# Issuing the loads of V from ScalarE's DMA queue instead of SyncE's, two of a period side by side

## The chip, the cores and the metric

One core of one Trainium2 chip runs the whole kernel. The metric is the device time of one execution in microseconds (us), so less is better. Engines are named as in the profile: PE is TensorE (PEld its weight loads), DVE is VectorE, ACT is ScalarE, POOL is GpSimd and SP is SyncE. A q behind an engine's name (SPq, ACTq) means its instruction queue, the sequencer that issues DMAs and waits for semaphores. The profile numbers the DMA queues: q1 holds what SP issues, q10 what ACT issues, and q8 is a queue of instruction fetches.

## What is computed

Two independent blocks A and B with the same shapes, whose results stand side by side in the output. In each, a projected query attends to a given K and V cache, and the heads are projected back:

```python
B, Sq, D = 16, 64, 640
H, Sk, Dh = 32, 512, 128
q = (x @ wq).reshape(B, Sq, H, Dh).transpose(0, 2, 1, 3)
scores = jnp.einsum("bhqd,bhkd->bhqk", q, k_cache) * (Dh ** -0.5)
p = softmax(scores, axis=-1)
o = jnp.einsum("bhqk,bhkd->bhqd", p, v_cache)
out = o.transpose(0, 2, 1, 3).reshape(B, Sq, H * Dh) @ wo
```

Everything is bf16. K and V of both blocks together take 256 loads of K and 256 loads of V, 512 KiB each, which is nearly all of the 292 MB that the kernel reads.

## The kernel before

The work is cut into 256 steps of two heads and two batches (an index m from 0 to 255); two steps make a *period*, of which there are 128. A period needs two loads of K (`kn_ring`, 9 slots) and two loads of V (`v_ring`, 5 slots of two halves: a period's two loads are the two batches of four heads). On top of that come the loads of the weights (`wq_sb`, `wo_sb`, 16 each, 640 KiB) and of x.

The order of every engine's instructions is written out by hand in `Cfg.PHASES`: for each engine a list of operations with an offset in steps and a time within the period. `build_plan` turns each into an `Op` with a time `ts`, in units of steps, and sorts each engine's list by it. An engine executes its list in that order. The operations that this document speaks of are

- on PE: `KX` transposes K (line 586), `QN` projects the queries of later steps (L603), `SM` computes the scores (L632), `TR2` transposes the probabilities (L670), `PV2` multiplies them with V (L694), `OP2` and `OX` project the output (L709, L719), `XT` transposes x (L804);
- on ACT: `EX` is the exponential with its row sum (L647, an ACTIVATE and a READ_ACCUMULATOR), `QEN` and `TA2` copy PSUM to SBUF (L619, L684), `OE4` copies the result of four PV products (L701), `OVP`, `OXP` and `XTE` are small copies (L727, L732, L833), and `ST` issues the DMA that stores a block of the output (L748), 16 times in all;
- on DVE: `MX` takes the row maximum (L641), `KE` and `TE2` copy (L593, L680); on POOL: `NM` normalizes the probabilities (L661).

A period of ACT runs OE4, EX, EX, EX, QEN, TA2, EX, and then the OE4 of the next one. OE4 waits for the second PV2 of the period, which is the last thing on PE in it; the first EX after it waits for DVE's MX.

Loads are ordered by the planner at the end of `build_plan` (lines 332 to 385). Each load gets a key, the time at which it may start: `LEAD` (5.37 steps) or `WLEAD` ahead of its first reader, and not before the slot is free. Sorted by that key, all loads go to SP's list (L384), K, V, x and weights mixed. The planner also computes, from estimated DMA costs, when the queue would come to each load, and takes the PE operation that runs at that time, but at the latest the one that runs `BEFORE` (3.88 steps) ahead of the load's first reader:

```python
i = bisect.bisect_right(pe_us, min(t_now, us(first - cfg.BEFORE))) - 1
if i > 0:
    paced.append((op, progs["pe"][i]))
```

`paced` makes the load wait for that PE operation: SP doesn't issue it until PE has come so far. So PE's progress paces the whole DMA queue. `em_LDKV` (L782) emits a load of K (L792) or V (L789). `prune_waits` leaves out each wait that another one implies. Each slot of a ring has a DMA semaphore of its own, on which PE waits before it reads the slot.

Of the kernel before, what the change touches and what calls it, by code (L numbers as in the profile page):

```python
# [15 lines left out]
class Cfg:  # L16
# [97 lines left out]
    OXH = False  # L114
    KTB = (6, 6)
    NWU = 32


class Op:
# [20 lines left out]
def build_plan(dims, cfg):  # L140
# [23 lines left out]
    progs = {e: [] for e in ENGINES}  # L164

    def mk(eng, kind, idx, reads, writes, ts, aux=None, dur=0.0):
        return Op(eng, kind, idx, reads, writes, dur=dur, aux=aux, ts=ts)
# [18 lines left out]
    for k in range(NPER - PPQ):  # L186
        u, i, hc = k // PPQ, k % PPQ // HG, k % HG
# [127 lines left out]
    for n, (k_lo, *templates) in enumerate(cfg.PHASES):  # L315
        k_hi = cfg.PHASES[n + 1][0] if n + 1 < len(cfg.PHASES) else 0
        for eng, template in zip(("pe", "act", "dve", "pool"), templates):
            for kind, off, sub, t in template:
                for m in range(2 * (k_lo % NPER) + off % 2, 2 * (k_hi % NPER or NPER), 2):
                    op = make_op(kind, m, sub, m - off + 2 * t / cfg.PERIOD)  # L320
# [8 lines left out]

    progs["pe"] = [mk("pe", "WU", -1, [("ident",)], [], -99, aux=cfg.NWU)] + progs["pe"]  # L330

# [6 lines left out]
    for ps_ in range(NPASS):  # L338
        for j in range(HG):
            ready = []  # L340
            if ps_:
                first = ("QN", (2 * ps_ - 1) * MPQ + j * MPG, 0)
                ready = [("QN", (2 * ps_ - 2) * MPQ + j * MPG + MPG - 2, 0)]
            else:
                first = ("QZ", 2 * j - 2, 0 if j > 1 else G) if j else ("QJ", 0, 0)
            add(ready, first, cfg.WLEAD, 0, "LDWQ", (ps_, j), [("wq", qslot(j))], (ps_, j))
            i = ps_ * HG + j
# [21 lines left out]
    def us(t):  # L369
        us_, a = min(t, 0) * cfg.STEP_US[0][1], 0  # L370
        for b, step in cfg.STEP_US:
            us_ += step * max(0, min(t, b) - a)
            a = b
        return us_

    pe_us = [us(op.ts) for op in progs["pe"]]
    paced = []
    t_now = cfg.START_US
    for key, first, _, op in sorted(loads, key=lambda e: e[:3]):
        t_now = max(t_now, us(key))  # L380
        i = bisect.bisect_right(pe_us, min(t_now, us(first - cfg.BEFORE))) - 1
        if i > 0:
            paced.append((op, progs["pe"][i]))
        progs["sp"].append(op)  # L384
        t_now += cfg.DMA_US[op.kind] * (op.aux[2] - op.aux[1] if op.kind == "LDX" else 1)

    counts = {}

    def sem_key(op):
# [113 lines left out]
def mha_kernel(nc, blocks, out, cfg=None):  # L503
# [12 lines left out]
    N1 = DN - N0  # L516

    progs, info = build_plan(dict(NBLK=NBLK, B=B, H=H, KT=KT), cfg)
    prune_waits(progs)
    NBP, SPB, NHALF = info["NBP"], info["SPB"], info["NHALF"]  # L520
# [413 lines left out]
```

## Time and profile before

| | |
|---|---|
| Median of 3 runs | 853.83 us (850.14 to 856.91) |
| The profiled execution's own time | 852.97 us |
| Its span (first to last instruction) | 851.0 us |
| Mean granted TensorE clock | 0.998 |
| DVE, ACT and POOL busy | 727.9, 644.7 and 417.1 us |
| Read from HBM | 292.03 MB, of which V is 134.2 MB |

The span is what the profiler sees; the 2 us beside it lie around it. The page's slices are 40 equal parts of the span, about 21 us each. "Released by" or "<-" behind an idle time names what ended the wait. "issue" is idle time in which the engine waited for nothing that the profile shows.

### The profile page before, as it was taken

How to read it: one execution, taken by the hardware profiler on the slowest of the kernel's cores; microseconds unless marked ns; L12 is line 12 of the kernel's file. 1: busy time of each engine (PE TensorE's matmuls, PEld its weight loads, DVE VectorE, ACT ScalarE, POOL GpSimd, SP SyncE). 2: the span in 40 equal slices, each digit the busy share in tenths (PEclk: the TensorE clock that was granted, in tenths of full speed). 3: DMA queues.
4: the chain of work that ended last, by engine and by line, in shares of the span. 5: the costliest groups of instructions: out<-in, count | busy, mean ns of one | idle time of the engine just before them, and what ended most of it. 6: DMA issues, size and time to landing. Idle time of an engine off the chain costs nothing.

```text
span 851.0 us, 38366 instructions
## 1 busy us (share of the span) xinstructions
PE 811.3 (95%) x17025; PEld 566.4 (67%) x17156; DVE 727.9 (86%) x1192; ACT 644.7 (76%) x1466; POOL 417.1 (49%) x518
## 2 busy tenths in 40 slices
PE   8999999999999999999999998999999999999996
PEld 5566676666666666666666666666666666666664
DVE  4688888888888898888899887988888989989994
ACT  2678877777777787777877877787887877778886
POOL 0355455454544554454554545455455455455553
PEclk9999999999999999999999999999999999999999
DMA  9999999999999999999999999999999999999992
GB/s 306 360 354 349 369 354 352 348 338 362 354 352 353 369 369 363 359 360 367 364 362 367 364 360 349 321 362 362 360 360 363 366 369 365 366 339 352 370 321 89
DMA packets 228438, 297.14 MB, mean 349 GB/s; under 512 B 9136, under 2 KB 162736, under 8 KB 228272
## 3 DMA queue, kind: packets, MB, share of 16 engines
q1 hardware_dynamic: 225968, 292.06, 100.3%
q8 instruction: 134, 2.20, 1.1%
q10 hardware_dynamic: 2304, 2.62, 0.9%
q14 instruction: 32, 0.26, 0.1%
HBM read 292.03 MB, written 2.62 MB: 346 GB/s over the span
## 4 chain that ended last, share of the span: by engine, by line
PE 89%; issue 3%; ACT 3%; DMA 2%; DVE 2%; SPq 0%; ACTq 0%
PE ps L586 17%; PE ps L694 15%; PE ps L603 15%; PE ps L632 14%; PE ps L670 13%; PE ps L709 12%; PE ps L719 3%; ACT p_ring L647 2%; DMA v_ring<-in_A_v_cache_dram 1%; DVE negmax L641 1%; ACT pT_ring L684 1%; DMA wq_sb<-in_A_wq_dram 1%; DVE ktp_ring L593 1%; PE ps L804 0%; PE ps L813 0%
## 5 line engine op out<-in xcount | busy, mean ns | idle before, releaser
L661 POOL TENSOR_SCALAR pn_ring<-p_ring,recip 128x512 bf16<-128x512 bf16 x512 | 416.4, 843 | 425.1 <-DVE recip L653 379.0
L647 ACT ACTIVATE p_ring<-ps,negmax 128x512 bf16<-128x512 f32 x512 | 349.0, 688 | 74.0 <-DVE negmax L641 68.5
L593 DVE COPY ktp_ring<-ps 128x2048 bf16<-128x2048 bf16 x256 | 312.1, 1219 | 56.3 <-PE ps L586 56.2
L641 DVE TENSOR_REDUCE negmax<-ps 128x1 f32<-128x512 f32 x512 | 328.3, 683 | 16.2 <-PE ps L632 8.5
L586 PEld LDWEIGHTS ps<-ident,kn_ring 64*128 64x128 bf16 x8192 | 136.8, 95 | 107.9 <-issue 96.4
L586 PE MATMUL ps<-ident,kn_ring 64*128 64x64 bf16 x8192 | 169.2, 191 | 3.3 <-issue 1.4
L603 PE MATMUL ps<-xT_sb,wq_sb 128*128 128x512 bf16 (+2 forms) x543 | 133.4, 372 | 19.0 <-issue 18.1
L670 PEld LDWEIGHTS ps<-ident,pn_ring 128*128 128x128 bf16 x2048 | 125.4, 98 | 38.8 <-ACT p_ring L647 7.2
L694 PE MATMUL ps<-pT_ring,v_ring 128*128 128x64 bf16 x4096 | 143.5, 194 | 2.8 <-issue 1.9
L701 ACT ACTIVATE oT_ring<-ps 128x512 bf16<-128x512 f32 x128 | 76.4, 597 | 91.7 <-PE ps L694 91.7
L684 ACT ACTIVATE pT_ring<-ps 128x1024 bf16<-128x1024 bf16 (+1 forms) x144 | 140.9, 987 | 3.0 <-DVE pT_ring L680 2.2
L670 PE MATMUL ps<-ident,pn_ring 128*128 128x128 bf16 x2048 | 138.9, 219 | 3.4 <-issue 1.6
L709 PE MATMUL ps<-wo_sb,oT_ring 128*128 128x512 bf16 x498 | 135.3, 379 | 4.0 <-issue 1.9
L632 PE MATMUL ps<-ktp_ring,qc_ring 128*64 128x512 bf16 x1024 | 135.5, 385 | 0.7 <-issue 0.7
L694 PEld LDWEIGHTS ps<-pT_ring,v_ring 128*128 128x128 bf16 x4096 | 128.2, 98 | 9.6 <-issue 2.4
L647 ACT ACTIVATION_READ_ACCUMULATOR p_ring<-ps,negmax 128x1 f32 x512 | 104.8, 205 | 0.0
L680 DVE COPY pT_ring<-ps 128x1024 bf16<-128x1024 bf16 (+1 forms) x128 | 82.5, 644 | 14.6 <-PE ps L670 14.1
L619 ACT ACTIVATE qc_ring<-ps 128x512 bf16<-128x512 f32 (+1 forms) x129 | 76.8, 596 | 21.5 <-PE ps L603 21.4
L603 PEld LDWEIGHTS ps<-xT_sb,wq_sb 128*128 128x128 bf16 x660 | 53.8, 98 | 54.0 <-issue 1.1
L632 PEld LDWEIGHTS ps<-ktp_ring,qc_ring 128*64 128x64 bf16 x1024 | 47.2, 109 | 34.1 <-issue 1.3
L709 PEld LDWEIGHTS ps<-wo_sb,oT_ring 128*128 128x128 bf16 x512 | 42.7, 98 | 25.0 <-ACT pT_ring L684 2.1
L653 DVE RECIPROCAL recip<-rowsum 128x2 f32<-128x2 f32 x256 | 39.8, 155 | 4.4 <-ACT p_ring L647 4.4
(21 smaller groups left out, 127.2 us busy)
## 6 DMA issues: line engine op xcount, KB each, us to landing
kn_ring<-in_A_k_cache_dram SPq DMA_DIRECT2D x128, 512.0 KB, 6.5
v_ring<-in_A_v_cache_dram SPq DMA_DIRECT2D x128, 512.0 KB, 6.8
kn_ring<-in_B_k_cache_dram SPq DMA_DIRECT2D x128, 512.0 KB, 6.3
v_ring<-in_B_v_cache_dram SPq DMA_DIRECT2D x128, 512.0 KB, 6.5
wq_sb<-in_A_wq_dram SPq DMA_DIRECT2D x8, 640.0 KB, 7.1
wo_sb<-in_A_wo_dram SPq DMA_DIRECT2D x8, 640.0 KB, 7.2
wq_sb<-in_B_wq_dram SPq DMA_DIRECT2D x8, 640.0 KB, 6.8
wo_sb<-in_B_wo_dram SPq DMA_DIRECT2D x8, 640.0 KB, 6.6
```

The source lines that it names most:

```text
L586: last = e.transpose(kt_ps[hs][:, 64 * t:64 * t + 64], kn_ring[r, m % NKB, t // 8, t % 8 * DH:(t % 8 + 1) * DH], ident[r, r])
L593: ins = e.tensor_copy(ktp_ring[:, ktslot(op.idx)], ps[:, b:b + 2, :].rearrange("p b s -> p (b s)").bitcast(BF16))
L603: last = e.matmul(dst[:, col:col + n], wq_sb[:, qslot(hh // G), kt, (hh % G) * DH:(hh % G + 1) * DH], xT_sb[:, kt, lo * 128:hi * 128], sta ...
L632: ins = e.matmul(s_bank(g)[64 * j:64 * j + 64, :], q[:, 64 * j:64 * j + 64], kt[:, sub, j], start=True, stop=True, tile_position=(0, 64 * j))
L641: ins = e.reduce_max(negmax[:, r:r + 1], s_bank(g), axis=AX.X, negate=True)
L647: ins = e.activation(p_ring[:, g % NP, :], s_bank(g), ACTF.Exp, bias=negmax[:, r:r + 1], scale=1.0, accum_out=rowsum[:, r:r + 1])
L661: ins = e.tensor_scalar(dst, src, recip[:, r:r + 1], 1.0, ALU.mult, ALU.mult)
L670: ins = e.transpose(pt_flat(m)[:, (4 * sub + t) * 128:(4 * sub + t + 1) * 128], pn_ring[:, g % NPN, t * 128:(t + 1) * 128], ident[:, :])
L680: ins = e.tensor_copy(*pt_copy(op.idx, op.aux))
L684: ins = e.activation(*pt_copy(op.idx, op.aux), ACTF.Copy)
L694: ins = e.matmul(qo_ps[:, col:col + 64], v_ring[:, m // 2 % NVP, j, 2 * (m % 2) + sub, t * DH:(t + 1) * DH], pT_ring[:, m % NT, sub, t, 64 ...
L709: ins = e.matmul(out_ps, oT_ring[:, m // 2 % NO, 2 * (m % 2) + sub, :], wo_sb[:, wslot(ps_, hh // G), hh % G, 0:N0], start=(hh == 0), stop ...
```

## The change

Loads of V (kind `LDV`) are no longer put on SP's list. They become operations of ACT, with a time of their own, and ACT's list is sorted again with them in it. K, x and the weights stay on SP as they are, in the same order and with the same waits.

```diff
+    VFIRST = 12
...
     for key, first, _, op in sorted(loads, key=lambda e: e[:3]):
         t_now = max(t_now, us(key))
         i = bisect.bisect_right(pe_us, min(t_now, us(first - cfg.BEFORE))) - 1
-        if i > 0:
-            paced.append((op, progs["pe"][i]))
-        progs["sp"].append(op)
+        if op.kind == "LDV":
+
+            op.eng = "act"
+            t = progs["pe"][max(i, cfg.VFIRST)].ts
+            op.ts = min(first - 0.01, max(key, t) if t < 4 else 2 * round(t / 2) + 0.02)
+            progs["act"].append(op)
+        else:
+            if i > 0:
+                paced.append((op, progs["pe"][i]))
+            progs["sp"].append(op)
         t_now += cfg.DMA_US[op.kind] * (op.aux[2] - op.aux[1] if op.kind == "LDX" else 1)
+    progs["act"].sort(key=lambda o: o.ts)
```

The time of a load of V is that of the PE operation that would have paced it, rounded to the nearest start of a period (an even number of steps) plus 0.02. Loads of V carry no paced wait; what holds them back is their place in ACT's list. In the built program that place is behind the last EX of a period and ahead of OE4 (or of the ST ahead of it) in 125 of 128 places. The lists of PE, DVE and POOL are unchanged. Counted in the built program, 96 places have two loads, 16 have three and 16 have one, and none of the 256 loads carries a wait for a semaphore: what ACT waited for earlier implies that the slot is free.

## The prediction

> **What bounds the kernel now.** First the page's busy times, slices and queues, then who waited for whom.
>
> ```profile
> span 851.0 us, 38366 instructions
> PE 811.3 (95%) x17025; PEld 566.4 (67%) x17156; DVE 727.9 (86%) x1192; ACT 644.7 (76%) x1466; POOL 417.1 (49%) x518
> ...
> DMA  9999999999999999999999999999999999999992
> GB/s 306 360 354 349 369 354 352 348 338 362 354 352 353 369 369 363 359 360 367 364 362 367 364 360 349 321 362 362 360 360 363 366 369 365 366 339 352 370 321 89
> ...
> q1 hardware_dynamic: 225968, 292.06, 100.3%
> q8 instruction: 134, 2.20, 1.1%
> q10 hardware_dynamic: 2304, 2.62, 0.9%
> ```
>
> Two things are full at once: PE is busy 95% of the span, and SP's queue q1 keeps the 16 DMA engines busy all the time at 350 to 369 GB/s. The waits say which one holds the other up:
>
> ```profile
> ACT oT_ring L701 <- PE ps L694: 91.7, 121, 1.8
> ACT p_ring L647 <- DVE negmax L641: 68.5, 127, 0.8
> ...
> PE ps L586 <- DMA v_ring<-in_A_v_cache_dram: 0.7, 1, 0.7
> ```
>
> PE waits for a load of V once, 0.7 us, just before its first use of V at 33.7 us, and never again. So DMA runs at its limit but PE sets the time. I cut the trace at the end of each second PV2. 74 periods have a QN and neither OX nor XT: the shortest is 6.11 us and so is their median. The 28 with an OX have 7.00 and 7.01. All time above the shortest of its class sums to 13.1 us from 57 us on; that and the first 34 us are all a better DMA could give back.
>
> More than half of the 13.1 us are gaps in the middle of an operation where nothing is waited for. In the chain that ended last, near 530 us:
>
> ```profile
> 529.18 0.69 PE ps L694 x20
> 529.87 1.06 issue
> 530.92 0.51 PE ps L694 x12
> ```
>
> PE stops after 20 of 32 matmuls. There are 12 such gaps between 160 and 835 us, 7.0 us together. They fit instruction fetch: q8 moved 134 packets of 16 KB for the 34181 instructions of PE and PEld, 255 each, the gaps stand at multiples of that, and 11 of the 12 end 1.32 to 1.62 us after a q8 packet ended.
>
> **The change part by part.** The sum is made against the profiled execution's own 852.97 us, 0.86 below the median of 853.83.
>
> *256 issues leave SP.* SP only issues, so its freed time is worth nothing. Loads of K lose no wait of their own.
>
> *256 issues join ACT, behind the last EX of a period.* One costs 0.34 to 0.44 us in the 16 rows of L748. In SP's rows, the second of two issues less than 0.1 us apart has a median of 0.47 and a mean of 0.61 us (71 cases after 40 us, longest 1.52). A pair then takes 0.37 + 0.04 + 0.47 = 0.88 us, a triple about 1.4. Does ACT's engine stand still meanwhile? This row of the ACT timeline decides:
>
> ```profile
> 788.88 0.69 ACT L647 ACTIVATE p_ring<-ps,negmax 128x512 bf16<-128x512 f32 x1
> 788.89 0.34 ACTq L748 DMA_DIRECT2D out_dram<-out_sb  x1
> 789.47 0.19 ACT L647 ACTIVATION_READ_ACCUMULATOR p_ring<-ps,negmax 128x1 f32 x1
> 789.75 0.60 ACT L701 ACTIVATE oT_ring<-ps 128x512 bf16<-128x512 f32 x1
> ```
>
> With nothing to wait for, the queue issues while EX runs; the same is seen at 812.67 and 835.92. Loads of V carry no wait and stand behind the same EX, so the first 0.8 us of a pair lie under it. Then come two idle times in every plain period:
>
> ```profile
> 624.25 0.71 ACT L647 ACTIVATE p_ring<-ps,negmax 128x512 bf16<-128x512 f32 x1
> 624.82 0.23 ACT L647 ACTIVATION_READ_ACCUMULATOR p_ring<-ps,negmax 128x1 f32 x1
> 625.85 0.60 ACT L701 ACTIVATE oT_ring<-ps 128x512 bf16<-128x512 f32 x1 [0.80 <-PE ps L694]
> ```
>
> 0.80 us before OE4, and 0.53 between OE4 and EX (which waits for DVE). Behind these wait QN (it needs OE4's bank; OE4 is done 0.70 us before) and TR2 (it needs EX's bank; behind an ST this EX starts 0.20 to 0.27 us later and the period takes 6.24, so about 0.1 us is to spare). Cover is 0.80 + 0.80 + 0.53 = 2.1 us; after an OX or XT it is about 1.6. Even a triple fits. I take 0. If the cover under EX is gone, the excess of pairs and triples over the two idle times, summed place by place, is 8.8 us with a second issue of 0.47 and 15.6 with 0.60. Bounds: 0 and +15.6.
>
> *The start.* V's first two loads are issued by SP at 15.8 and 21.9 us and land at 27.1 and 33.6; PV2 wants them at 32.7. On ACT they go out near 15.5. The 0.7 us wait goes; next in line are a K and a WQ load that land 3.2 and 3.7 us ahead of their readers, while 1 MB of V, 2 x 1.45 us at the rate at which landings follow each other, cuts in. That fits. I take -0.7; bounds -0.9 (all of that wait) and +1.
>
> *V's loads meet K's in the DMA engines.* In before, a load takes 6.3 to 6.8 us from issue to landing, in order. When an ST runs on q10, the packet records show its 1280-byte packets 94 ns apart beside q1's 1024-byte ones, where the two take 55 and 46: the engines alternate single packets of the two queues and lose nothing. In a pair each engine has 64 packets of V. Beside a period's 40 of K and weights (84 ns for K's 2048 bytes) that is 64 x 0.046 + 40 x 0.084 = 6.3 us, plus about 2.5 us from issue to first packet (2.1 to 3.3 for the STs under load): 8.8 us. By where ACT and PE stand in this trace, two thirds of V's loads will go out 10.8 to 13.3 us before their PV2, a sixth 18 or more, 12 of 256 less than 10.8. For most, 2 us and more are left: I take 0. If every packet of V had one of K beside it, 64 x 0.130 + 2.5 = 10.8 us, and the 34 periods with a lead under 11.6 would be at the edge; 0.35 us in each is +12. Bounds: 0 and +12.
>
> *Instruction fetch.* From the trace, a q8 packet starts on average 2.9 us after PE enters the block ahead of it (0.2 to 5.2), against 0.3 at the first fetch. With the spare time of each of the 126 fetches, extra latency costs: 0.2 us more, 5.6 us in all; 0.3, 9.4; 0.5, 18.7; 1.0, 50. Less latency gives up to 7.0 back. In the fetches during STs the latency is 1.5 to 4.0, as elsewhere, so I take 0; but an ST has 9 packets per engine, a pair of V 64. Bounds: -7.0 and +50. [...]
>
> Sum: 852.97 - 0.7 + 0 + 0 + 0 = 852.3 us.
>
> **The rivals.**
>
> *Instruction fetch falls behind (slower).* If each queue keeps packets of its own in flight inside an engine, a fetch waits behind those of two queues. For: latency is ten times that of the first fetch, and margins are thin. Against: STs don't show it. It decides from +0.3 us of latency on (+9.4 us); my price is +0.5: 852.3 + 18.7 = 871.0, and 902 at +1.0.
> [...]
>
> *ACT's issues aren't covered (slower).* [...] +8.8 to +15.6: 861 to 868. Against: the row at 788.88.
>
> *V comes late (slower).* As above, +12: 864.
>
> *Two queues feed the engines better (faster).* During STs both queues together move 340 to 380 GB/s, mostly over 360, against 350 to 364 in most 100 us windows. Then fetches come sooner, and of the 13.1 us above the shortest periods some goes; all of it would give 852.3 - 13.1 = 839.2. 844.4 needs 60% of it. Against: DVE and ACT waits in there have nothing to do with DMA.
>
> [...]
>
> **How the numbers follow.** My forecast, all four terms small, 0.45 (own range 846 to 860). Fetch 0.20, ACT uncovered 0.10, V late 0.12, faster 0.13. Within 1% is 844.4 to 861.5, about what a measurement of this kernel can tell from no change. Faster by over 1%: 0.13. Within: 0.45 plus 0.02 of the uncovered ACT at its lower price, 0.47. Slower: the rest, 0.40. The range 843 to 875 takes in the forecast, both cheap rivals and fetch to +0.6 us; left out are a dearer fetch (about 0.12) and the deepest gain (0.05).
>
> **What would show it.** After: q10 with about 137 MB; issues of V on ACTq inside EX's time; 0.80 before OE4 still there, or smaller where issues are long. "DMA v_ring" among PE's waits means V comes late. More or longer "issue" gaps inside PE's operations, or periods over 6.11 with no other wait, mean fetch. "ACT oT_ring L701" idle by "issue" means ACT isn't covered. I am wrong if a full second queue does to fetches what an ST's few packets can't.

## The result, and the profile after

| | before | after |
|---|---|---|
| Median | 851.99 us | 877.56 us (873.88 to 882.2, 4 runs) |
| Ratio, with its 95% interval | 1 | 1.0297 (1.0219 to 1.0374) |
| The profiled execution's own time | 852.97 us | 875.14 us |
| Its span | 851.0 us | 873.1 us |

The median of before is that of the runs beside the changed kernel. The change costs 3.0%, against a forecast of no change. The changed kernel's lines stand nine further down: PV2 is L703, KX L595, QN L612, EX L656, OE4 L710, ST L757 and the load of V L798.

The page of the changed kernel, busy times, slices and queues:

```profile
span 873.1 us, 38366 instructions
PE 817.6 (94%) x17025; PEld 568.2 (65%) x17156; DVE 728.8 (83%) x1192; ACT 645.3 (74%) x1466; POOL 418.1 (48%) x518
...
GB/s 271 364 333 352 353 325 342 358 366 354 343 353 352 326 348 369 354 325 365 355 356 362 367 346 361 325 336 334 353 354 350 359 351 330 372 338 340 370 312 89
...
q1 hardware_dynamic: 90800, 157.83, 52.0%
q10 hardware_dynamic: 137472, 136.86, 47.5%
q8 instruction: 134, 2.20, 1.1%
```

The change did what it says: q10 now moves 137 MB. The work of ACT, DVE and POOL is nearly unchanged (ACT 645.3 against 644.7 us). PE is busy 6.3 us longer, about half of it, by the estimate for cut operations below, at the cuts. DMA still moves up to 372 GB/s, but from the second to the 38th slice nine are under 340, where before has three. So most of the time lost isn't work. Where does PE stand still? The waits of the changed kernel (engine, line, releaser: us in total, times, longest):

```profile
ACT oT_ring L710 <- issue: 8.5, 7, 2.0
PE ps L703 <- issue: 6.9, 12, 1.4
PE ps L595 <- issue: 6.8, 19, 1.0
...
PE ps L612 <- ACT oT_ring L710: 2.3, 4, 1.0
PE ps L718 <- ACT oT_ring L710: 2.2, 3, 1.2
...
PE ps L703 <- DMA v_ring<-in_B_v_cache_dram: 0.3, 1, 0.3
```

The same lines of before:

```profile
PE ps L694 <- issue: 1.9, 3, 1.1
...
PE ps L586 <- issue: 1.4, 5, 0.5
...
PE ps L709 <- ACT oT_ring L701: 0.7, 1, 0.7
```

PE's stops for "issue" in PV2 and KX grew from 3.3 to 13.7 us, its waits for OE4 from 0.7 to 4.5 us, and V is late once. The first kind in the chain of the changed kernel that ended last:

```profile
383.90 0.89 PE ps L703 x27
384.80 1.41 issue
386.21 0.31 PE ps L703 x5
386.52 0.98 PE ps L641 x8
```

The 32 matmuls of a period's two PV2 are cut in two, as in before at 529.87, only longer. A *fetch gap* here is idle time of PE of more than 0.19 us, after 50 us, that ends 1.05 to 1.8 us after a q8 packet and stands where a block begins. Such gaps went from 11 (6.2 us) to 30 (15.2 us). Blocks are 255 recorded instructions of PE and PEld apart in before and after (256 in the traces that record more, such as sp_pairs). The profile says "issue" at all but one of these places; that they are fetches I infer from that spacing and from q8. A cut also costs beside its gap: these 32 matmuls run 0.89 + 0.31 = 1.20 us, and from the start of uncut ones to the next operation it is 1.04 (302.32 to 303.36 in before), so 0.16 us more. A second count takes that in, and the shorter stops as well: from the start of one matmul to the start of the next across such a boundary, less the usual distance, wherever that is over 0.1 us. By it, 30 stops cost 12.2 us in before and 51 cost 26.6 in after, 14.4 more.

The spans of the two profiled executions differ by 22.1 us (the medians by 25.6; the profiled one of after is the second fastest of four). The parts found in the traces:

| Part | us |
|---|---|
| First four periods (the fourth starts at 60.8 instead of 57.3 us) | 3.5 |
| Fetch gaps, 15.2 - 6.2 | 9.0 |
| Cuts and shorter stops at fetches, 14.4 - 9.0 | 5.4 |
| PE's waits for OE4, 4.5 - 0.7 | 3.8 |
| V late | 0.3 |

They sum to 22.0. The last four make 18.5, and the time above the shortest period of each class grew by 18.6 us (13.2 to 31.8).

### The profile page after: what moved, and what is told of

Its sections match the earlier page's. It is cut to its first block, busy times and chain, and to the rows that moved or that the text cites. A ratio compares the mean times of both kernels' runs of the same rounds, so it can differ in the third digit from the quotient of the medians.

```text
span 873.1 us, 38366 instructions
## 1 busy us (share of the span) xinstructions
PE 817.6 (94%) x17025; PEld 568.2 (65%) x17156; DVE 728.8 (83%) x1192; ACT 645.3 (74%) x1466; POOL 418.1 (48%) x518
## 4 chain that ended last, share of the span: by engine, by line
PE 84%; ACT 5%; issue 5%; DVE 3%; DMA 2%; ACTq 1%; POOL 0%; SPq 0%; DVEq 0%
PE ps L595 16%; PE ps L612 14%; PE ps L703 14%; PE ps L641 13%; PE ps L679 12%; PE ps L718 11%; ACT p_ring L656 3%; PE ps L728 3%; DMA v_ring<-in_B_v_cache_dram 2%; DVE negmax L650 2%; ACT pT_ring L693 1%; DMA wq_sb<-in_A_wq_dram 1%; DVE ktp_ring L602 1%; ACT qc_ring L628 0%; ACTq L798 0%
## 5 line engine op out<-in xcount | busy, mean ns | idle before, releaser
L656 ACT ACTIVATE p_ring<-ps,negmax 128x512 bf16<-128x512 f32 x512 | 349.2, 688 | 68.8 <-DVE negmax L650 67.1
L595 PEld LDWEIGHTS ps<-ident,kn_ring 64*128 64x128 bf16 x8192 | 137.6, 95 | 114.1 <-issue 104.2
L595 PE MATMUL ps<-ident,kn_ring 64*128 64x64 bf16 x8192 | 172.3, 191 | 8.3 <-issue 6.8
L710 ACT ACTIVATE oT_ring<-ps 128x512 bf16<-128x512 f32 x128 | 76.4, 597 | 112.1 <-PE ps L703 103.5
L612 PE MATMUL ps<-xT_sb,wq_sb 128*128 128x512 bf16 (+2 forms) x543 | 134.6, 375 | 20.6 <-issue 17.5
L703 PE MATMUL ps<-pT_ring,v_ring 128*128 128x64 bf16 x4096 | 144.1, 193 | 8.2 <-issue 6.9
L703 PEld LDWEIGHTS ps<-pT_ring,v_ring 128*128 128x128 bf16 x4096 | 128.3, 98 | 17.0 <-issue 9.8
L656 ACT ACTIVATION_READ_ACCUMULATOR p_ring<-ps,negmax 128x1 f32 x512 | 104.8, 205 | 0.0
L612 PEld LDWEIGHTS ps<-xT_sb,wq_sb 128*128 128x128 bf16 x660 | 54.8, 99 | 55.8 <-ACT oT_ring L710 1.9
```

Source lines behind the costliest of these rows:

```text
L595: last = e.transpose(kt_ps[hs][:, 64 * t:64 * t + 64], kn_ring[r, m % NKB, t // 8, t % 8 * DH:(t % 8 + 1) * DH], ident[r, r])
L612: last = e.matmul(dst[:, col:col + n], wq_sb[:, qslot(hh // G), kt, (hh % G) * DH:(hh % G + 1) * DH], xT_sb[:, kt, lo * 128:hi * 128], sta ...
L656: ins = e.activation(p_ring[:, g % NP, :], s_bank(g), ACTF.Exp, bias=negmax[:, r:r + 1], scale=1.0, accum_out=rowsum[:, r:r + 1])
L703: ins = e.matmul(qo_ps[:, col:col + 64], v_ring[:, m // 2 % NVP, j, 2 * (m % 2) + sub, t * DH:(t + 1) * DH], pT_ring[:, m % NT, sub, t, 64 ...
```

## The experiments

Each ratio is to runs of the kernel before on the same chip. "Fetch latency" is the mean time from PE's entry into one such block to the start of the q8 packet that, by this reading, brings the next: 2.95 us in before, 3.48 in after. Taking a block to begin three records earlier or later moves these means by 0.1 to 0.3 us, so small differences between them say little. The expectations below go by a count of gaps that also took in waits with another cause which happened to end as long after a packet; in after, three waits for OE4 of 2.0 us made it 33 gaps and 17.2 us.

### Pairs without the second queue, and the second queue without V

sp_pairs leaves V on SP's queue but paces it as the change does:

```diff
+        if op.kind == "LDV":
+            t = progs["pe"][max(i, cfg.VFIRST)].ts
+            t = max(key, t) if t < 4 else 2 * round(t / 2) - 0.2
+            i = bisect.bisect_right([o.ts for o in progs["pe"]], t) - 1
...
+    for _, _, op, i in sorted(spl, key=lambda e: e[:2]):
```

> V stays on SP's queue, but its loads are ordered and paced as in the change: two (sometimes three or one) next to each other at the end of a period. One queue carries all data. If the second queue is the cause (fetches of PE's instructions late, +11.0 us of gaps, and ACT's issues, +4 to 7.6 us): 0.995 to 1.010 of the kernel before, PE's gaps behind a fetch about 6 us as there, mean fetch latency near 2.95 us. If the bunching of V's loads is the cause, whichever queue: 1.02 to 1.03, gaps near 17 us, latency near 3.5 us.

Measured: 1.022 (1.0171 to 1.027). The profile's queues and PE's waits (PV2 is L707 here, KX L599):

```profile
q1 hardware_dynamic: 225968, 292.06, 99.3%
q8 instruction: 134, 2.20, 1.0%
```

```profile
PE ps L599 <- issue: 9.0, 17, 1.0
...
PE ps L707 <- issue: 3.7, 9, 1.2
```

All loads are on q1, and the gaps are there all the same: 33 of them, 16.1 us, latency 3.27 us. By the count from start to start, stops at fetches cost 13.9 us more than in before, and the span is 14.6 us longer. So three quarters of the loss need no second queue. In this kernel a load of K that stands behind a load of V in SP's list waits for V's place, so K's times shift too; the run doesn't separate that from the pairs.

act_tiny is the kernel before with one more DMA of 64 bytes on ACT at each place where the change puts a load of V:

```diff
+            progs["act"].append(mk("act", "LDZ", op.idx, [], [("z", op.idx)], t))
...
+            ins = e.dma_start(z_sb[0:16, op.idx, :], blocks[0][0][0, 0:16, 0:2])
```

> The kernel before with 256 extra DMAs of 64 bytes (results unused), issued by ACT at the places where the change puts V's loads; V itself stays on SP. It has ACT's issues without the data. If ACT's issues cost nothing by themselves: 0.995 to 1.005. If they carry the 7.6 us that the fetch and the start don't explain: 1.006 to 1.012, with periods of 7.36 instead of 7.01 us behind an OX. If they carry all of the loss: 1.03. Fetch gaps should stay near 6 us by every theory that blames a deep second queue for them.

Measured: 1.0019 (0.9988 to 1.005), with 11 fetch gaps of 5.3 us together. ACT spends 129 us of issue time on its 272 DMAs, against 143 in after, and PE waits for OE4 1.3 us in all (0.7 in before). So the issues as such were all but covered: 0.6 us more of these waits, and a time that can't be told from before's.

act_start_sp gives ACT only the loads of V after the start:

```diff
-        if op.kind == "LDV":
+        if op.kind == "LDV" and progs["pe"][max(i, cfg.VFIRST)].ts >= 4:
```

> The change with V's first loads (those whose place is before step 4) left on SP, so that the start is the old one. If the 3.5 us that the first four periods lost come from V cutting in: 1.022 to 1.027, fourth period starting near 57.3 us instead of 60.8. If they are scatter of the start or the slower first weight load: about 1.03, as the change.

Measured: 1.0297 (1.0263 to 1.0332), the same as the whole change, though its fourth period starts at 57.5 us, as in before. The 3.5 us that the start of after lost in its profiled run are not what the 3% are made of.

act_one_of_two gives ACT every second load of V; each half of a slot then has a semaphore of its own:

```diff
-        if op.kind == "LDV":
+        if op.kind == "LDV" and op.idx % 2 == 0:
...
-            return ("d_" + op.kind[2:].lower(), op.writes[0][1])
+            return ("d_" + op.kind[2:].lower(),) + op.writes[0][1:]
```

> Only the first of each period's two loads of V goes through ACT, the second stays on SP with its paced wait (each half of a slot has its own semaphore here, so PE waits for two instead of one). Second queue half as deep, one issue on ACT per place. If depth of the second queue delays fetches: about half the loss, 1.010 to 1.018, fetch gaps 9 to 13 us. If two busy queues suffice: 1.02 to 1.03. If ACT's pairs and triples of issues are the cause: under 1.005, since one issue is covered.

Measured: 1.0265 (1.022 to 1.031), 36 fetch gaps of 22.8 us. Half the loads on ACT cost nearly as much as all; the loss doesn't go with the number of issues on ACT.

### Fewer bytes, and other times

sp_halfV and act_halfV load only the first half of each V slot after the ring's first round, on the queues of before and after. From then on the other half of a slot keeps older data, so half of V is left out of what they compute. The edit is the same in both:

```diff
-                ins = e.dma_start(v_ring[:, m // 2 % NVP, m % 2], src)
+                    ins = e.dma_start(v_ring[:, m // 2 % NVP, m % 2, :, 0:2 * DH], src[:, :, 0:2 * DH])
```

> The kernel before, but from the sixth period on each load of V brings only half of its data (the other half of the slot keeps older data, so the result isn't the reference's). Issues and waits stay, DMA has a fifth less to do and is no longer full. Fetches should come in time: fetch gaps under 2 us, 0.985 to 0.993. If the gaps have nothing to do with the load on DMA: 6 us of gaps and 1.00.

> The change with the same halved loads of V. ACT's 256 issues stay, the full DMA queues don't. If the loss of the change lies in a full DMA (fetches, and issues that stall because of it): within 0.4% of the same kernel on SP. If ACT's issues cost by themselves, in pairs and triples with full descriptor counts: 0.5 to 1% slower than that one.

Measured: 0.9916 (0.9886 to 0.9946) on SP and 0.9969 (0.9936 to 1.0002) on ACT. The pages of the two, sp_halfV first:

```profile
span 842.0 us, 38366 instructions
...
GB/s 302 357 348 266 297 254 272 279 272 272 286 294 287 278 287 274 285 291 279 280 289 308 272 267 287 250 280 285 278 275 284 300 274 283 272 252 277 300 214 45
...
q1 hardware_dynamic: 225968, 227.58, 86.7%
```

```profile
span 844.0 us, 38366 instructions
...
q1 hardware_dynamic: 90800, 157.83, 57.0%
q10 hardware_dynamic: 137472, 72.37, 29.5%
```

PE's waits in act_halfV:

```profile
PE ps L612 <- issue: 17.7, 111, 0.2
ACT oT_ring L710 <- issue: 3.4, 4, 1.6
...
PE ps L703 <- issue: 0.4, 1, 0.4
...
PE ps L718 <- ACT oT_ring L710: 2.0, 3, 0.8
...
PE ps L612 <- ACT oT_ring L710: 0.9, 3, 0.3
```

The first line is the 0.16 us before a QN that every plain period has, in before too (18.1 us). Long stops are almost gone: no fetch gap in sp_halfV and one of 0.4 us in act_halfV. With some 280 GB/s instead of 350 the loss of the change goes: sp_halfV is faster than the kernel before, and act_halfV's interval reaches just to 1. The two lie 0.5% apart, the low end of what was expected if ACT's issues cost by themselves. What is left on ACT is the wait for OE4: 2.9 us here, 0.7 in sp_halfV.

sp_earlier and sp_later keep everything on SP and shift all issues by 1.5 us:

```diff
-        i = bisect.bisect_right(pe_us, min(t_now, us(first - cfg.BEFORE))) - 1
+        i = bisect.bisect_right(pe_us, min(t_now, us(first - cfg.BEFORE)) - 1.5) - 1
```

(and + 1.5 in the other)

> The kernel before, all loads on SP in the same order, each paced 1.5 us of the planner's time (0.44 steps) earlier. Nothing is bunched, the queue is just deeper: about 5.4 loads in flight instead of 4.5. If PE's instruction fetches wait behind what is in flight (depth): latency 3.3 to 3.5 us instead of 2.95, fetch gaps 12 to 18 us instead of 6.2, 1.007 to 1.015. If only side-by-side loads of V do it (bunching): gaps 5 to 8 us, 0.995 to 1.004.

> The same with each load paced 1.5 us later: about 3.6 loads in flight. Depth: latency 2.2 to 2.6 us, fetch gaps 0 to 3 us, 0.993 to 0.998, if V isn't late (its least spare time before PV2 was 0.9 us in the kernel before; a DMA that runs dry would show as waits of PE for v_ring and 1.00 to 1.02). Bunching: gaps 5 to 8 us, 0.997 to 1.003.

Measured: 1.0019 (0.9986 to 1.0052) and 1.0017 (0.998 to 1.0054). I wanted more and fewer loads in flight this way and didn't get them: 4.60 and 4.53 on average between 60 and 800 us, against 4.47. The shift went into the time that a load lies ready before its reader: for V 7.5 and 4.9 us on average, against 6.3 in before. So these two say that a shift of all issue times by 1.5 us didn't matter here, and nothing on loads in flight. They also rule out that V's earlier issue is the cause: sp_earlier issues V 14.4 us ahead of its PV2 on average and sp_pairs 14.2 (before 13.0, after 15.4), but only sp_pairs loses 2.2%.

### The spacing

act_single puts one load of V a step on ACT instead of two a period; act_spread_late does so a step later:

```diff
-            op.ts = min(first - 0.01, max(key, t) if t < 4 else 2 * round(t / 2) + 0.02)
+            op.ts = min(first - 0.01, max(key, t) if t < 4 else 2 * round(t / 2) + 0.02 - (op.idx % 2 == 0))
```

(act_spread_late: `+ (op.idx % 2)`)

> V stays on ACT's queue, but the bunching is undone: the first load of a pair goes out one step (about 3.1 us) earlier, between QEN and TA2, the second stays. Two queues are as busy as in the change. If bunching causes the late fetches: fetch latency back to 2.8 to 3.1 us, gaps 5 to 9 us, 1.002 to 1.010. If two deep queues cause them, bunched or not: latency about 3.5, gaps 15 us and more, 1.02 to 1.03.

> As the one before, but the second load of a pair goes out one step later and the first stays. Bunching: fetches as in the kernel before, 1.002 to 1.012, where the second load, with a lead of about 9 us against 8.3 from issue to landing, may come late and cost some waits for v_ring. Two queues: 1.02 to 1.03 as the change.

Measured: 1.0182 (1.0144 to 1.022) with 29 fetch gaps of 13.7 us, and 1.0172 (1.0135 to 1.0209) with 16 of 7.3. The second isn't a clean test, since its loads come too late. PE's waits in act_spread_late:

```profile
PE ps L703 <- DMA v_ring<-in_B_v_cache_dram: 8.9, 5, 5.9
...
PE ps L703 <- DMA v_ring<-in_A_v_cache_dram: 5.3, 3, 2.7
```

These 14.2 us of waits for V are the larger part of the 22.5 us that the profiled execution, the slowest of its four, loses. This is what the rival "V comes late" looks like; after has 0.3 us of it.

sp_fours is sp_pairs with four loads side by side every two periods, sp_even spaces the loads of before more evenly from step 40 on:

```diff
-            t = max(key, t) if t < 4 else 2 * round(t / 2) - 0.2
+            t = max(key, t) if t < 4 else 4 * (2 * round(t / 2) // 4) - 0.2
```

```diff
+            even = max(even + cfg.DMA_US[op.kind] / 3.2, first - 5.2)
+            i = bisect.bisect_right(pe_ts, even) - 1
```

> V on SP's queue, four loads (two periods' worth) side by side every second period; one queue. A larger dose of bunching. If fetches wait behind a bunch: more late ones than with pairs in the half of the periods that follow a bunch, latency there over 4 us, 1.025 to 1.05. If pairs lose for another reason (their place at the period's end, or K's loads held up behind the pacing waits of V): 1.015 to 1.025, as pairs.

> V on SP's queue, all loads in the order of the kernel before but paced evenly: each at least the planner's own DMA cost (in steps of 3.2 us) behind the one before. The spacing of two loads then scatters by 0.13 steps instead of 0.21. If side-by-side loads set the fetch latency: 2.5 to 2.9 us, fetch gaps 2 to 5 us, 0.993 to 0.999. If what is left of the gaps in the kernel before has another cause: 0.998 to 1.004.

Measured: 1.0195 (1.0164 to 1.0226) with 36 fetch gaps of 16.0 us, and 1.0029 (1.0007 to 1.0051) with 16 of 6.4. Fours are no worse than pairs, and more even spacing is no better than the planner's. Both miss what was expected if side-by-side loads set the latency: a larger dose didn't cost more, and sp_even, where a load follows another within 0.6 us 27 times instead of 86, gained nothing. That sp_fours loses by fetches all the same is shown by the count from start to start: 15.7 us more than in before, for a span 15.5 us longer.

sp_single is sp_pairs with act_single's one load a step, and act_asis is the change without the rounding, so that each load of V has the planner's time on ACT's list:

```diff
-            t = max(key, t) if t < 4 else 2 * round(t / 2) - 0.2
+            t = max(key, t) if t < 4 else 2 * round(t / 2) - 0.2 - (op.idx % 2 == 0)
```

```diff
-            op.ts = min(first - 0.01, max(key, t) if t < 4 else 2 * round(t / 2) + 0.02)
+            op.ts = min(first - 0.01, max(key, t))
```

> V on SP's queue, one load a step at the places at which the kernel with one load a step on ScalarE has them, so without pairs and without a second queue. If the second queue is what that kernel's 1.8% come from, this one is at 1.000 to 1.006 with fetch gaps of 5 to 8 us. If what costs is that V is issued at fixed places, which fall beside K's issues, so that more loads are in flight when a fetch is asked for, this one is at 1.010 to 1.018 too, with gaps of 11 to 15 us.

> V from ScalarE's queue, each load at the place in time that the planner gives it, without rounding to the start of a period: the second queue alone, with K and V spaced as in the kernel before. If the second queue costs by itself, 1.012 to 1.02 with gaps of 10 to 15 us. If the spacing is what counts, 1.000 to 1.008 with gaps below 10 us; ScalarE's own operations can then shift an issue by about 1 us, which is why I do not expect exactly 1.000.

Measured: 1.0162 (1.0129 to 1.0195) and 1.0118 (1.0093 to 1.0143). PE's waits in sp_single, where q1 again carries 292 MB:

```profile
PE ps L707 <- issue: 5.5, 12, 1.3
PE ps L599 <- issue: 4.2, 10, 1.0
...
PE ps L722 <- ACT oT_ring L714: 0.7, 1, 0.7
```

With these the table of queue by spacing is full. "Close" counts, between 60 and 800 us, the loads that another follows within 0.6 us, of some 490; "6+" the fetches, of some 120, that are asked for while six or more loads are in flight (a load of weights counted as 1.25).

| V is issued | on SP's queue | close, 6+ | on ACT's queue | close, 6+ |
|---|---|---|---|---|
| at the planner's times | 1 (before) | 86, 6 | 1.0118 (act_asis) | 135, 29 |
| one a step, fixed places | 1.0162 (sp_single) | 124, 31 | 1.0182 (act_single) | 144, 53 |
| two a period | 1.022 (sp_pairs) | 163, 21 | 1.0297 (after) | 192, 54 |

Read down the first column: on one queue, giving up the planner's spacing costs 1.6%, pairs 2.2%, with intervals that overlap. Read across the lower two rows: the queue adds 0.2 and 0.8%, again with overlapping intervals, so that it adds anything isn't shown. Neither count orders the six kernels by itself: sp_pairs has fewer fetches under "6+" than sp_single and loses more. act_asis isn't the second queue alone, as I had meant it to be. V's issues stand in ACT's list and go out when ACT gets there, and more loads than in before are issued next to another (135 against 86).

The latency of the fetches grew with the loads in flight. In before it is 2.26 us with three to four loads in flight, 2.68 with four to five, 3.20 with five to six and 3.45 with more (6 fetches). In after the last class holds 54 of 121 fetches and has 3.95 us. Before's four latencies, weighted by after's classes, give 3.14 us: of the 0.53 us that latency grew by, 0.2 come from more loads in flight at a fetch. For the rest, the place behind a pair counts: in after a fetch took 4.1 to 4.3 us when asked for 1 to 3 us behind a pair's issue, and 2.1 to 2.7 beyond 5 us.

## Why the prediction was wrong, point by point

**The step that failed: "so I take 0" for instruction fetch.** The rival for it happened at about its price: latency grew by 0.53 us, for +0.5 the prediction has +18.7, and 14.4 us came. With ACT's 3.8 and the start's 3.5 it makes up most of the 22.8 us between the forecast of 852.3 and the profiled 875.14; the median, 877.56, lies above the range of 843 to 875. The bounds of the term (-7 to +50) held. The rival's +0.5 was a guess of mine that no trace had shown. The mistake was to let the STs decide. An ST puts 9 packets on each engine and a pair 64, which the prediction itself says, and the nearer row was the latency's own dependence on what is in flight in the trace of before, 2.26 to 3.45 us, which the prediction doesn't use. That row would have shown the direction and not the size: with after's classes it gives 0.2 us, which the prediction prices at 5.6. How long PE stood still for fetches hung on the spacing of the loads and on how much they move: 15.2 us of fetch gaps in after, 6.2 in before, none in sp_halfV.

**The rival's reason was mostly wrong.** It was that "each queue keeps packets of its own in flight", a matter of two queues. sp_pairs and sp_single lose 2.2 and 1.6% with one. The change had two parts, the queue and the pairing, and I priced the pairing only as issue time on ACT and as lateness of V, never by what a burst does to the fetches on q8, which in after took 4.1 to 4.3 us when asked for 1 to 3 us behind a pair's issue. Whether the queue's own part is zero, the 0.2 and 0.8% with their overlapping intervals don't decide.

**ACT's issues: 0 predicted, 3.8 us measured.** The bounds (0 to +15.6) held. In plain periods the cover is as argued. In the ACT timeline of after:

```profile
157.02 1.19 ACTq L798 DMA_DIRECT2D v_ring<-in_A_v_cache_dram  x2
157.54 0.71 ACT L656 ACTIVATE p_ring<-ps,negmax 128x512 bf16<-128x512 f32 x1
158.11 0.23 ACT L656 ACTIVATION_READ_ACCUMULATOR p_ring<-ps,negmax 128x1 f32 x1
159.14 0.60 ACT L710 ACTIVATE oT_ring<-ps 128x512 bf16<-128x512 f32 x1 [0.80 <-PE ps L703]
```

This pair takes 1.19 us instead of my 0.88 (the median of 97 pairs is 0.95, the longest 2.16), and OE4 still has its 0.80 us of idle time before it. The first issue even starts before the EX that stands ahead of it in ACT's list. "Even a triple fits" was wrong when issues are long:

```profile
85.74 0.69 ACT L656 ACTIVATE p_ring<-ps,negmax 128x512 bf16<-128x512 f32 x1 [0.70 <-DVE negmax L650]
85.74 1.86 ACTq L798 DMA_DIRECT2D v_ring<-in_A_v_cache_dram  x2
86.32 0.19 ACT L656 ACTIVATION_READ_ACCUMULATOR p_ring<-ps,negmax 128x1 f32 x1
87.63 0.53 ACTq L798 DMA_DIRECT2D v_ring<-in_A_v_cache_dram  x1
88.21 0.60 ACT L710 ACTIVATE oT_ring<-ps 128x512 bf16<-128x512 f32 x1 [1.70 <-issue]
```

The first two take 1.86 us, the third issue ends at 88.16, and OE4 starts at 88.21. That is the line "ACT oT_ring L710 <- issue", seven times in after, and the "PE <- ACT oT_ring" behind it. PE's waits for OE4, 4.5 us in after and 0.7 in before, are 1.3 with loads of 64 bytes in the same places (act_tiny) and 2.9 with half loads (act_halfV).

**V late: right.** Landing took 8.3 us in the median instead of 6.6, and the estimate for a pair was 8.8. One load left PE waiting.

**The start: wrong in sign, in one run's scatter.** The wait for V went, but the fourth period starts at 60.8 us, 3.5 later, where the bound was +1. Until 9.43 us PE waits 3.7 us for the first load of weights (0.9 in before). That load is issued at 1.8 us in both traces and lands at 9.4 instead of 7.4, long before ACT issues its first load of V at 18.9 us (forecast: near 15.5). The granted clock over the first 20 us is 0.74 instead of 0.91, and the first 20 matmuls of L612 take 2.31 us instead of 1.29. Over the experiments the fourth period starts between 57.3 and 62.1 us, with 62.1 and the same 0.74 in act_tiny, whose loads of V are those of before, so this is scatter of one run more than an effect of the change.

**What stays open.** Whether the 0.8% between pairs on SP and pairs on ACT is all OE4's waits (3.8 us are 0.4%) or also a second queue's own share in a fetch's wait; the intervals of the two ratios overlap. Why act_halfV lies 0.5% above sp_halfV with 2.2 us more of such waits, which are 0.3%. And what it is about a load's place that delays a fetch: loads in flight give 0.2 of the 0.53 us, fours cost no more than pairs, and a more even spacing than the planner's gained nothing.

## What to carry to other kernels

Here, with the DMA engines busy throughout at about 350 GB/s, the spacing of loads alone was worth 1.6% (sp_single) and 2.2% (sp_pairs). In sp_pairs 13.9 of the 14.6 us came through stops that I read as instruction fetches of PE and that no semaphore shows. In a kernel like this one, look for stops in the middle of an operation at a fixed count of instructions, 255 recorded ones here. Price a change of issue times also by what it does to the loads in flight at a fetch, in the trace of before, and not by bandwidth or the loads' own deadlines alone. Here that gives the direction and less than half of the size. Two edits that come as one, here a queue and a pairing, want a price each.

## What the runs showed of the hardware

- Shifting all issues by 1.5 us either way changed neither the loads in flight (4.53 to 4.60, 4.47 in before) nor the time (1.0017 and 1.0019).
- A fifth less DMA traffic (sp_halfV, 227.58 MB on q1 against 292.06) took every fetch gap away on one queue (11 of 6.2 us in before) and made the kernel 0.8% faster, so the gaps of before are a price of its full DMA, too.
- In after, DMA issues ran beside the ACTIVATE that stands ahead of them in ACT's list, and a pair started before it did (157.02 against 157.54 us). Where they reached past ACT's idle time they held the next operation up (an issue that ended at 88.16 us, OE4 at 88.21): beside ACT's 143 us of issues, PE waited 3.8 us more for OE4.
- Bursts twice as large (sp_fours, 1.0195) cost no more than pairs (sp_pairs, 1.022), though SP then spends 410 us on issues, against 273.
